# Attention and MLP in one kernel: batch 1's input is loaded earlier and its first work moved into the opening

## The chip, the cores and the metric

The kernel runs on one core of one Trainium2 chip. The time is device microseconds from the first to the last instruction of one execution, as the median of several runs; the profile is of one execution, whose span was 203.0 us.

## The reference

The inputs are `x` (8 batches, 8 heads, 512 rows, 64 columns), `state` (8 batches, 8 heads, 32 rows, 64 columns), and the weights `w_in` (512 x 2048) and `w_out` (2048 x 512), all float32. For each batch and head:

```
scores  = x @ state.T / 8            # 512 x 32
a       = softmax(scores)            # over the 32 state rows
xread   = a @ state                  # 512 x 64
scores2 = state @ x.T / 8            # 32 x 512
sread   = softmax(scores2) @ x       # 32 x 64
```

`xread` and `sread` are joined along the rows (544 rows a batch), the heads are laid side by side (512 columns), and the resulting 4352 x 512 matrix goes through an MLP with exact Gelu:

```
out = gelu(rows @ w_in) @ w_out      # 4352 x 512, float32
```

## The kernel before, in words

Everything is computed in bfloat16 with float32 sums. The eight batches follow one another; the order of all instructions on all engines is written out by hand, so each engine runs its instructions in exactly the order in which the program's lines issue them, and waits only for data and buffers.

For a batch `b`, `xtr` transposes x (64 columns of a head at a time, two heads into one 128-row tile) into `xT`. `state_prep` transposes the state and puts it in block form into `sbd`. `scores(b, half)` multiplies the two and takes exp on ScalarE into `e`; `norm` sums and divides on VectorE into `a`; `atr` transposes `a` into `AT`. Since `xread @ w_in` is `a @ (state @ w_in)`, the kernel first forms P = state @ w_in for 512 columns of w_in at a time (`p_mm`, then `p_copy`: one half is copied out of PSUM by ScalarE, the other by VectorE). A `burst` does `p_mm` for two or three such pieces and then their copies; `pmat` does one.

`M(k)` is one block of the first MLP layer: block `k % 16` of batch `k // 16`, 128 of the 2048 hidden columns for all 512 rows, two matmuls of 128x512 and a Gelu on ScalarE into `g`. `mm2_m(0, m)` and `U(u)` are pieces of the second layer, four matmuls of 128x512 each that add into the four output banks `op`. `mm2_m(0, m)` needs Gelu block `m` of batch 0 and rows `128 m` to `128 m + 127` of w_out. From batch 2 on, the second layer uses sums of operands (`g_sum`, `X`), which is not touched here.

`sread(b)` computes the second attention from the same `e` and from `xo`, a copy of x with columns of ones that give the softmax sums (`ones0` fills it for batch 0, `rearr_ones` for the others); `sread_out` divides on VectorE into `srm`; `srt` transposes that into `XSR`, where the state rows of all batches are gathered for the end of the kernel.

PSUM has eight banks. Four are the pool `ps_f`, handed out in turn for first-layer blocks `hp`, P pieces `p_ps`, transposes, scores `pt` and `sr`; the next user of a buffer waits until the last one's result has been copied out. The other four, `o0` to `o3` of `ps_o`, hold the output sums `op` and, in the opening, small things.

The loads of weights, of the states of batches 1 to 7 and of x of batches 1 to 7 are issued by GpSimd and convert float32 to bfloat16 on the way. Their order is that of the calls: `load_w_in`, `load_w_out` and `load_st` at the top, then `load_x(1)` in the middle of the opening, then `load_rest()`. x of batch 0 comes by other queues.

The opening (lines 955 to 1014) does attention and the first four blocks of batch 0 while the first weights arrive; `keep_warm` fills waits there with matmuls whose result nobody uses. `first` is the two halves of those four blocks, into the tiles `hps`. After them comes a list of units by hand, lines 1013 to 1096, in which batch 0's second layer is interleaved with batch 1's attention and first blocks, M(16) to M(31), and with batch 2's attention.

Of the kernel before, what the change touches and what calls it, by code (L numbers as in the profile page):

```python
# [10 lines left out]
BF16 = mybir.dt.bfloat16  # L11
# [6 lines left out]
def kernel(  # L18
# [17 lines left out]
    SJ = S // 128  # L36
# [11 lines left out]
    ps_f = ctx.enter_context(tc.tile_pool(name="ps_f", bufs=4, space=PSUM))  # L48
    ps_o = ctx.enter_context(tc.tile_pool(name="ps_o", bufs=1, space=PSUM))
# [51 lines left out]
    def load_w_in(f0, f1):  # L101
        for t in range(2):
            nc.gpsimd.dma_start(
                out=w_in_bf[64 * t:64 * t + 64, :, f0:f1],
                in_=moe_w_in[256 * t:256 * t + 256, f0:f1].rearrange("(c d) f -> d c f", c=HC),
            )
# [3 lines left out]
    def load_w_out(m0, m1):  # L110
        nc.gpsimd.dma_start(out=w_out_bf[:, m0:m1, :], in_=w_out_r[:, m0:m1, :])

    def load_x(b):
        xb = xin.tile([128, H, SJ * D], BF16, name="xb", tag="xb")
        nc.gpsimd.dma_start(out=xb, in_=xr[b])
        xbs[b] = xb

    def load_st(b0, b1):
        nc.gpsimd.dma_start(
            out=st_bf[:, b0:b1, :, :].rearrange("q b t d -> q (b t) d"),  # L120
            in_=st_rows[:, b0:b1, :, :].rearrange("q b t d -> q (b t) d"),
        )

    load_w_in(0, 256)
    load_w_in(256, 512)
    load_w_out(0, 2)
    load_st(1, 2)
    load_w_out(2, 4)
    load_w_in(512, 1024)

# [23 lines left out]
    def state_prep(b0, b1):  # L154
        n = b1 - b0
        ps = ps_f.tile([128, n, HC, NS], BF16, name="st_ps", tag="f")
        for b in range(b0, b1):
            nc.tensor.transpose(
                ps[:, b - b0, :, :].rearrange("p c n -> p (c n)"),
                st_bf[:, b, :, :].rearrange("q t d -> q (t d)"),  # L160
                ident,
            )
        for t in range(2):
            nc.vector.tensor_copy(
                out=sbd[64 * t:64 * t + 64, b0:b1, :, 32 * t:32 * t + 32].rearrange(
                    "d b c n -> d (b c) n"
                ),
                in_=ps[64 * t:64 * t + 64, :, :, :].rearrange("d b c n -> d (b c) n"),
            )
# [34 lines left out]
    def begin(b):  # L204
        A = Att()
        atts[b] = A
        A.x4 = x4s[b % 2]
        A.xo = xos[b % 2]
        if b > 0:
            A.xT = att.tile([128, SJ, HC, 128], BF16, name="xT", tag="xT")  # L210

    def begin_e(b):
        A = atts[b]
        A.e = att.tile([128, SJ * 2, HC * NS], BF16, name="e", tag="e")
        A.a = att.tile([128, SJ * 2, HC * NS], BF16, name="a", tag="a")
# [12 lines left out]
    def rearr_ones(b):  # L228
        A = atts[b]
        eng = nc.vector if b < 2 else nc.gpsimd  # L230
        src = xbs[b].rearrange("p (t c) (j d) -> p t c j d", t=2, d=D)
        for t in range(2):
            eng.tensor_copy(  # L233
                out=A.xo[:, :, :, 2 + 64 * t:66 + 64 * t].rearrange("p j c d -> p c j d"),
                in_=src[:, t],
            )
# [9 lines left out]
    def ones0(q):  # L246
        nc.vector.tensor_copy(
            out=atts[0].xo[:, :, q % 2 * 2:q % 2 * 2 + 2, 2 + q // 2 * 64:66 + q // 2 * 64],
            in_=x0b[:, q, :, :, :],
        )  # L250
# [8 lines left out]
        copy(out=xT0[:, q, :, :], in_=ps)  # L259


    def xtr(b, cs):
        A = atts[b]
        xv = xbs[b].rearrange("p (t c) (j d) -> p j c t d", t=2, d=D)
        ps = ps_f.tile([128, len(cs), SJ, 128], BF16, name="xT_ps", tag="f")
        for i, c in enumerate(cs):
            for j in range(SJ):
                for t in range(2):
                    nc.tensor.transpose(ps[64 * t:64 * t + 64, i, j, :], xv[:, j, c, t, :], ident)  # L269
        nc.vector.tensor_copy(  # L270
            out=A.xT[:, :, cs[0]:cs[0] + len(cs), :].rearrange("p j c n -> p c j n"), in_=ps
        )
# [47 lines left out]
    def scores(b, half):  # L320
        A = atts[b]
        if half == 0:
            begin_e(b)
        pt = ps_f.tile([128, SJ, 2, 2, NS], FP32, name="pt", tag="f")
        for ci in range(2):
            c = 2 * half + ci
            for j in range(SJ):
                nc.tensor.matmul(  # L328
                    pt[:, j, :, ci, :],
                    lhsT=A.xT[:, j, c, :],  # L330
                    rhs=sbd[:, b, c, :],
                    start=True,
                    stop=True,
                )
        nc.scalar.activation(  # L335
            out=A.e[:, :, 64 * half:64 * half + 64],
            in_=pt.rearrange("p j t c n -> p (j t) (c n)"),
            func=AF.Exp,
            scale=scale,
        )  # L340
# [40 lines left out]
    def sread(b):  # L381
        A = atts[b]
        A.sr = ftile([128, 2, 65], "sr")
        for t in range(2):
            for j in range(SJ):
                for c in range(HC):
                    nc.tensor.matmul(  # L387
                        A.sr[32 * c:32 * c + 32, t, :],
                        lhsT=A.e[:, 2 * j + t, 32 * c:32 * c + 32],
                        rhs=A.xo[:, j, c, 1 + 65 * t:66 + 65 * t],  # L390
                        start=(j == 0),
                        stop=(j == SJ - 1),
                    )

    def sread_out(b):
        A = atts[b]
        A.srm = att.tile([128, 2, D], BF16, name="srm", tag="srm")
        flat = A.sr.rearrange("q t d -> q (t d)")
        inv = att.tile([128, 2], FP32, name="inv", tag="inv")
        nc.vector.reciprocal(out=inv, in_=flat[:, 0:130:129])  # L400
        nc.vector.tensor_tensor(
            out=A.srm,
            in0=flat[:, 1:129].rearrange("q (t d) -> q t d", t=2),
            in1=inv[:, :].to_broadcast((128, 2, D)),
            op=ALU.mult,
        )

    def srt(b):
        A = atts[b]
        ps = ps_f.tile([128, HC, NS], BF16, name="srT", tag="f")  # L410
        nc.tensor.transpose(  # L411
            ps.rearrange("p c n -> p (c n)"), A.srm.rearrange("q t d -> q (t d)"), ident
        )
        nc.vector.tensor_copy(out=XSR[:, :, :, b], in_=ps)  # L414
# [29 lines left out]
    def burst(chunks, b_read=None):  # L444
        done = []
        first = len(chunks) < 4 and b_read is not None
        if first:
            sread(b_read)
        for i, (b, f) in enumerate(chunks):
            done.append((b, f, p_mm(b, f, ftile if i < 2 else otile)))  # L450
        for x in done[:2]:
            p_copy(*x)
        if b_read is not None and not first:
            sread(b_read)
        for x in done[2:3]:
            p_copy(*x)
        if b_read is not None:
            sread_out(b_read)
        for x in done[3:]:
            p_copy(*x)  # L460
# [65 lines left out]
    def mm2_m(b, m):  # L526
        for j in range(SJ):
            if m == 0:
                ops[b, j] = otile([128, d_model], "op")
            nc.tensor.matmul(  # L530
                ops[b, j],
                lhsT=gs[b][:, m, j * 128:(j + 1) * 128],
                rhs=w_out_bf[:, m, :],
                start=(m == 0),
                stop=(m == MC - 1),
            )
# [364 lines left out]
    def M(*ms):  # L901
        for m in ms:
            mm1(m // MC, m % MC)
# [70 lines left out]
    keep_warm(6)  # L974
    sums0(1)
    norm0(0)
    load_x(1)
    scores0(3)
    sums0(2)
    sums0(3)  # L980
# [22 lines left out]
    first(0, (0, 1))  # L1003
    atr(0, (1,))
    nc.vector.tensor_copy(out=Ps[0][:, 1, 256:512], in_=late[1])
    for q in range(4):
        ones0(q)
    first(0, (2, 3))
    first(1, range(4))
    for m in range(4):  # L1010
        nc.scalar.activation(out=gs[0][:, m, :], in_=hps[m], func=AF.Gelu)
    turn[0] = 3
    mm2_m(0, 0)
    mm2_m(0, 1)
    state_prep(1, 2)
    mm2_m(0, 2)
    burst([(1, 0), (0, 1)])
    mm2_m(0, 3)
    M(4, 5)
    M(6)  # L1020
    begin(1)
    xtr(1, (0, 1))
    xtr(1, (2, 3))
    sread(0)
    sread_out(0)
    M(7)
    scores(1, 0)
    scores(1, 1)
    srt(0)
    mm2_m(0, 4)  # L1030
    mm2_m(0, 5)
    rearr_ones(1)
    mm2_m(0, 6)
    norm(1, 0)
    sread(1)
    pmat(0, 2)
    sread_out(1)
    norm(1, 1)
    mm2_m(0, 7)
    M(8, 9)  # L1040
    M(10, 11)
    mm2_m(0, 8)
    atr(1)
    mm2_m(0, 9)
    burst([(1, 1), (0, 3)])
    mm2_m(0, 10)
    M(16, 17)
    M(12, 13)
    srt(1)
    M(14, 15)  # L1050
# [7 lines left out]
    U(13)  # L1058
    state_prep(2, B)
    U(14)  # L1060
    M(18, 19)
    U(15)
    burst([(2, 0), (2, 1), (2, 2)])
    U(16)
# [110 lines left out]
    b = B - 1  # L1175
# [40 lines left out]
```

The softmax here doesn't subtract the row's maximum and nothing guards it: scores larger than these inputs give would overflow.

## Time and profile before

| What | Value |
|---|---|
| Time, median of three runs | 204.88 us (204.70 to 205.03) |
| Span of the profiled execution | 203.0 us |
| Granted TensorE clock | 1.000 |
| VectorE busy | 149.1 us, 73% |
| ScalarE busy | 134.7 us, 66% |
| GpSimd busy | 67.0 us, 33% |
| Read from and written to HBM | 17.30 MB and 8.91 MB |

Busy time of an engine is the time that its instructions were in work, and the share is of the span. PE is TensorE's matmuls, PEld its weight loads, which overlap them. In the page's second part the span is cut into 40 slices of 5.1 us, and a digit is the busy share of a slice in tenths. In a list of instructions, `out<-in` names the tiles, and what stands in brackets at the end of a line is how long the engine sat idle before it and what ended that. The end of a matmul is modelled, so its start is the better mark. For a load, the time to landing counts from its issue. Lines L530 and L515 are the second layer's matmuls (`mm2_m` and `mm2`), L995 and L489 the first layer's, L424 P, L269 the transposes of x, L387 `sread`, L328 the scores, L158 and L411 the transposes of the state and of `srm`.

### The profile page before, as it was taken

What the parts mean: (1) busy time and instruction counts of PE and PEld (TensorE: products, weight loads), DVE (VectorE), ACT (ScalarE), POOL (GpSimd) and SP (SyncE); (2) the same over time, 40 slices, a digit from 0 to 9 for tenths busy, and PEclk for the clock granted to TensorE, in tenths of its full rate; (3) what the DMA queues carried; (4) which work ended last, traced back from release to release, by engine and by line L of the source; (5) the groups of instructions that cost most, each with busy time, mean ns of one, the idle gap of its engine ahead of it and who ended that gap; (6) DMA issues with size and microseconds to landing.
All of it is one profiled execution on the core that took longest, in us unless ns stands there. A gap on an engine that the chain in (4) does not pass through costs nothing.

```text
span 203.0 us, 4784 instructions
## 1 busy us (share of the span) xinstructions
PE 198.0 (98%) x1987; PEld 128.1 (63%) x1987; DVE 149.1 (73%) x246; ACT 134.7 (66%) x237; POOL 67.0 (33%) x73
## 2 busy tenths in 40 slices
PE   7899999999999999999999999999999999999994
PEld 2444544444454577766776677667776787878893
DVE  2954863866767679877897787768778988895883
ACT  3785678479894879666967697587847576864120
POOL 8963610742860315370626602430220002200000
PEclk9999999999999999999999999999999999999999
DMA  6999999789475908952693405380109001040225
GB/s 194 196 178 203 207 197 192 121 236 179 83 95 149 224 0 105 158 171 38 77 182 116 93 3 120 107 140 3 52 0 194 15 3 52 3 155 0 55 98 162
DMA packets 40325, 23.14 MB, mean 114 GB/s; under 512 B 21872, under 2 KB 38384, under 8 KB 40304
## 3 DMA queue, kind: packets, MB, share of 16 engines
q1 hardware_dynamic: 25616, 14.36, 29.6%
q0 software_dynamic: 14000, 8.10, 29.2%
q10 hardware_dynamic: 688, 0.39, 0.6%
q8 instruction: 15, 0.25, 0.5%
q14 instruction: 6, 0.05, 0.1%
HBM read 17.30 MB, written 8.91 MB: 129 GB/s over the span
## 4 chain that ended last, share of the span: by engine, by line
PE 94%; DMA 2%; DVE 1%; ACT 1%; issue 0%
PE xp L585 35%; PE hp L489 27%; PE op L515 9%; PE op L530 5%; PE p_ps L424 4%; PE sp L791 3%; PE rp L857 3%; PE xp L696 2%; DMA st_f<-in_state_dram 2%; PE pt L328 2%; PE sr L387 1%; PE hp L995 1%; PE aT_ps L369 1%; PE xT_ps L269 0%; DVE x0b L241 0%; PE warm_ps L148 0%
## 5 line engine op out<-in xcount | busy, mean ns | idle before, releaser
L496 ACT ACTIVATE g<-hp 128x512 bf16<-128x512 f32 x124 | 66.9, 602 | 28.4 <-PE hp L489 23.0
L489 PE MATMUL hp<-AT,P 128*128 128x512 bf16 x248 | 63.2, 379 | 0.0
L585 PEld LDWEIGHTS <-gsum 128*128 128x128 bf16 x448 | 43.3, 98 | 10.4 <-issue 1.9
L579 DVE TENSOR_TENSOR gsum<-g 128x2048 bf16<-128x2048 bf16 x30 | 38.7, 1305 | 0.1
L489 PEld LDWEIGHTS <-P 128*128 128x128 bf16 x248 | 22.8, 98 | 21.9 <-issue 2.2
L585 PE MATMUL xp<-ws,gsum 128*128 128x256 bf16 x256 | 30.6, 273 | 0.0
L436 DVE CAST P<-p_ps 128x512 bf16<-128x512 f32 x31 | 20.0, 684 | 5.4 <-PE p_ps L424 5.4
L585 PE MATMUL xp<-ws,g 128*128 128x256 bf16 x192 | 22.9, 273 | 0.0
L585 PE MATMUL xp<-w_out_bf,gsum 128*128 128x256 bf16 x192 | 22.8, 273 | 0.0
L435 ACT CAST P<-p_ps 128x512 bf16<-128x512 f32 x31 | 16.8, 597 | 7.2 <-PE p_ps L424 6.3
L585 PEld LDWEIGHTS <-g 128*128 128x128 bf16 x192 | 18.8, 98 | 4.1
L639 POOL TENSOR_TENSOR u<-s,oh 128x512 f32<-128x512 f32 x5 | 6.6, 1315 | 41.1 <-ACT oh L636 41.1
L515 PE MATMUL op<-w_out_bf,g 128*128 128x512 bf16 x80 | 19.7, 379 | 0.0
L233 POOL COPY xo<-xb 128x1024 bf16<-128x1024 bf16 x12 | 15.5, 1325 | 12.6 <-PE sr L387 12.6
L223 POOL COPY x<-xb 128x1024 bf16<-128x1024 bf16 x12 | 12.3, 1055 | 8.9 <-DMA xb<-in_x_dram 8.9
L604 POOL TENSOR_TENSOR v<-q,oh 128x512 f32<-128x512 f32 x5 | 7.2, 1431 | 20.4 <-ACT oh L641 20.4
L515 PEld LDWEIGHTS <-g 128*128 128x128 bf16 x80 | 7.6, 98 | 9.3 <-issue 0.8
L348 DVE TENSOR_REDUCE cs<-e 128x16 f32<-128x512 bf16 x14 | 9.5, 678 | 4.5 <-ACT e L335 4.5
L530 PE MATMUL op<-w_out_bf,g 128*128 128x512 bf16 x48 | 11.8, 380 | 0.0
L351 DVE TENSOR_TENSOR a<-e,ics 128x512 bf16<-128x512 bf16 x14 | 10.3, 735 | 0.5
L414 DVE COPY XSR<-srT 128x128 bf16<-128x128 bf16 x8 | 5.7, 758 | 6.6 <-PE srT L411 6.6
L424 PE MATMUL p_ps<-w_in_bf,sbd 64*32 64x512 bf16 x248 | 10.1, 382 | 0.0
(127 smaller groups left out, 234.7 us busy)
## 6 DMA issues: line engine op xcount, KB each, us to landing
xb<-in_x_dram POOLq DMA_DIRECT2D x7, 512.0 KB, 6.0
out_dram<-oh SPq DMA_DIRECT2D x13, 256.0 KB, 2.5
out_dram<-osb SPq DMA_DIRECT2D x10, 256.0 KB, 3.3
out_dram<-oh SPq DMA_DIRECT2D x5, 512.0 KB, 2.7
w_out_bf<-in_moe_w_out_dram POOLq DMA_DIRECT2D x8, 256.0 KB, 10.0
w_in_bf<-in_moe_w_in_dram POOLq DMA_DIRECT2D x6, 256.0 KB, 10.4
x0f<-in_x_dram SPq DMA_DIRECT2D x3, 256.0 KB, 4.1
w_in_bf<-in_moe_w_in_dram POOLq DMA_DIRECT2D x4, 128.0 KB, 4.5
```

The source lines that it names most:

```text
L223: nc.gpsimd.tensor_copy(out=A.x4[:, :, :, 64 * t:64 * t + 64].rearrange("p j c d -> p c j d"), in_=src[:, t],)
L233: eng.tensor_copy(out=A.xo[:, :, :, 2 + 64 * t:66 + 64 * t].rearrange("p j c d -> p c j d"), in_=src[:, t],)
L351: nc.vector.tensor_tensor(out=A.a[:, :, hs].rearrange("p g (c n) -> p g c n", n=NS), in0=e4, in1=ics[:, :, :].to_broadcast((128, G, 2, NS) ...
L424: nc.tensor.matmul(ps[t][32 * c:32 * c + 32, :], lhsT=sbd[64 * t:64 * t + 64, b, c, 32 * t:32 * t + 32], rhs=w_in_bf[64 * t:64 * t + 64, c ...
L435: nc.scalar.copy(out=dst[:, 0, :], in_=ps[0])
L436: nc.vector.tensor_copy(out=dst[:, 1, :], in_=ps[1])
L489: nc.tensor.matmul(hp, lhsT=Ps[b][:, t, m * 128:(m + 1) * 128], rhs=atts[b].AT[:, :, t, :], start=(t == 0), stop=(t == 1),)
L496: nc.scalar.activation(out=gs[b][:, m, :], in_=hp, func=AF.Gelu)
L515: nc.tensor.matmul(ps, lhsT=gs[b][:, m, j * 128:(j + 1) * 128], rhs=w_out_bf[:, m, :], start=(m == 0), stop=(m == MC - 1),)
L530: nc.tensor.matmul(ops[b, j], lhsT=gs[b][:, m, j * 128:(j + 1) * 128], rhs=w_out_bf[:, m, :], start=(m == 0), stop=(m == MC - 1),)
L579: nc.vector.tensor_tensor(out=t, in0=g_q(b, h0, k0), in1=g_q(b, h1, k1), op=op)
L585: nc.tensor.matmul(ps[:, j - js[0], :], lhsT=lhs[:, m, 128 * j:128 * j + 128], rhs=rhs[:, m, :], start=(first and j == js[0] and m == 0), ...
```

## The change

It brings batch 1's attention forward. x of batch 1 is loaded right behind the first 512 columns of w_in, ahead of the first rows of w_out. Its transposes and those of its state are issued before batch 0's second layer begins, one of the two groups of transposes through the bank `o2` of the other pool; its scores come after two units of the second layer instead of after seven blocks. Batch 1's normalisation and `atr` follow earlier, so that its first blocks, M(16) to M(19), can run among batch 0's, as other work to put between the units of the second layer. `sread(0)`, its division and two of the `ones0` copies move with it. No instruction is added or left out.

```diff
     load_w_in(0, 256)
     load_w_in(256, 512)
+    load_st(1, 2)
+    load_x(1)
     load_w_out(0, 2)
-    load_st(1, 2)
     load_w_out(2, 4)
     load_w_in(512, 1024)
...
-    def xtr(b, cs):
+    def xtr(b, cs, pool=ps_f, tag="f"):
...
-        ps = ps_f.tile([128, len(cs), SJ, 128], BF16, name="xT_ps", tag="f")
+        ps = pool.tile([128, len(cs), SJ, 128], BF16, name="xT_ps", tag=tag)
...
     norm0(0)
-    load_x(1)
     scores0(3)
...
-    for q in range(4):
-        ones0(q)
+    ones0(0)
+    ones0(1)
     first(0, (2, 3))
     first(1, range(4))
     for m in range(4):
         nc.scalar.activation(out=gs[0][:, m, :], in_=hps[m], func=AF.Gelu)
+    begin(1)
+    xtr(1, (0, 1), ps_o, "o2")
+    xtr(1, (2, 3))
+    state_prep(1, 2)
+    ones0(2)
+    ones0(3)
     turn[0] = 3
     mm2_m(0, 0)
     mm2_m(0, 1)
-    state_prep(1, 2)
+    scores(1, 0)
+    scores(1, 1)
     mm2_m(0, 2)
+    sread(0)
+    sread_out(0)
     burst([(1, 0), (0, 1)])
+    norm(1, 0)
     mm2_m(0, 3)
     M(4, 5)
-    M(6)
-    begin(1)
-    xtr(1, (0, 1))
-    xtr(1, (2, 3))
-    sread(0)
-    sread_out(0)
-    M(7)
-    scores(1, 0)
-    scores(1, 1)
-    srt(0)
+    M(6, 7)
+    norm(1, 1)
     mm2_m(0, 4)
     mm2_m(0, 5)
     rearr_ones(1)
+    srt(0)
     mm2_m(0, 6)
-    norm(1, 0)
+    atr(1)
     sread(1)
     pmat(0, 2)
     sread_out(1)
-    norm(1, 1)
     mm2_m(0, 7)
+    M(16, 17)
     M(8, 9)
     M(10, 11)
     mm2_m(0, 8)
-    atr(1)
+    M(18, 19)
     mm2_m(0, 9)
     burst([(1, 1), (0, 3)])
     mm2_m(0, 10)
-    M(16, 17)
     M(12, 13)
     srt(1)
     M(14, 15)
...
     U(14)
-    M(18, 19)
     U(15)
```

## The prediction

> **What bounds the kernel now.** I read the page first, then the chain of waits in order of time, then the timeline of the first 45 us, then the loads one by one.
>
> The page says that one engine carries the span:
>
> ```profile
> PE 198.0 (98%) x1987; PEld 128.1 (63%) x1987; DVE 149.1 (73%) x246; ACT 134.7 (66%) x237; POOL 67.0 (33%) x73
> ...
> PE   7899999999999999999999999999999999999994
> ```
>
> TensorE is full from the third slice to the last. The change neither adds nor removes a matrix instruction, so the time can only move by what TensorE idles. The chain of waits for the stretch that the diff touches (start, length, what):
>
> ```profile
> 12.29 1.04 PE hp L995 x4
> ...
> 13.35 1.90 PE op L530 x8
> 15.25 0.06 PE st_ps L158
> 15.31 0.86 PE op L530 x4
> 16.17 0.56 PE p_ps L424 x16
> 16.73 0.97 PE op L530 x4
> ...
> 17.70 1.51 PE hp L489 x6
> 19.21 1.01 PE xT_ps L269 x32
> ```
>
> A 128x512 matmul costs 0.216 us in a stream (`op x4` is 0.86). From 12.29 us on, every piece starts where the one before ends. What idle there is hides in pieces that are too long (six matmuls are 1.30 us, the piece of `hp` is 1.51), and the timeline gives it with its releaser in brackets:
>
> ```profile
> 13.35 1.41 PEld L530 LDWEIGHTS <-g 128*128 128x128 bf16 x8 [0.53 <-ACT g L1011]
> ...
> 17.70 0.10 PEld L489 LDWEIGHTS <-P 128*128 128x128 bf16 x1 [0.50 <-ACT P L435]
> ...
> 21.22 0.29 DVE L401 TENSOR_TENSOR srm<-sr,inv 128x128 bf16<-128x128 f32 x1
> 21.56 0.10 PEld L411 LDWEIGHTS <-srm 128*128 128x128 bf16 x1
> ...
> 27.69 0.54 PEld L530 LDWEIGHTS <-g 128*128 128x128 bf16 x4 [0.41 <-ACT g L496]
> ```
>
> In lost stream time (start minus the start of the matmul before, minus 0.216) these are: 0.20 us at 13.35 (the first Gelu), 0.21 at 17.70 (P of the burst still being copied), 0.14 at 21.57 (the transpose of srm), 0.08 at 27.7 and 0.04 at 33.7. So 0.67 us is all that any reordering can win in this stretch; from 34 us to the end I find only the 0.1 us steps at each change of tile shape.
>
> The loads are the second resource. Slices 1 to 8 of the page move about 200 GB/s, and each load's issue and time to landing can be had one at a time, here those of w_out blocks 2 and 3 and of x of batch 1:
>
> ```profile
> L111 POOL DMA_DIRECT2D w_out_bf<-in_moe_w_out_dram x1: 753/753/753, 7.1 to 7.1; - x1
> DMA to landing us min/median/max: 6.4/6.4/6.4
> ...
> L115 POOL DMA_DIRECT2D xb<-in_x_dram x1: 962/962/962, 9.0 to 9.0; - x1
> DMA to landing us min/median/max: 9.6/9.6/9.6
> ```
>
> Issue plus landing, in order: w_in 256-512 at 9.6 and 10.3 us, w_out 0-1 at 11.6, state 1 at 11.8, w_out 2-3 at 13.5, w_in 512-1024 at 14.8 and 16.0, x1 at 18.6, w_out 4-5 at 19.9, 6-7 at 21.3. They land one after another, 256 KB per 1.3 us: a line in which order is everything.
>
> **What the Trainium skill says.** *DMA: Bandwidth & Descriptors*, "Issuing engines are not separate DMA queues": all loads end on the same 16 engines. The trace agrees: landings follow the order of issue, 1.3 us apart. *PSUM — Partial Sum Buffer*, "Engine vs sequencer instructions": Scalar and Vector queues are strict FIFO and matmuls start in program order; so a matmul that waits holds all behind it, as at 17.70. *ScalarE: Activation LUTs*, "What ACT_TABLE_LOAD costs": about 1283 ns a load, the same as the 1283 ns here.
>
> **The change part by part.**
>
> *Load order.* x1 (512 KB) goes ahead of w_out 0-1, w_out 2-3 and w_in 512-1024. x1 now ends at the byte position (512 + 32 + 512 KB) at which w_out 2-3 ended before: 13.5 us. By rate it is 10.3 + 0.2 (state) + 2.6 (x1's own, 18.6 minus 16.0) = 13.1. I take 13.3 and keep both ends. The three it overtakes come 2.6 later at most, and less by the same token: w_out 0-1 at 14.6 (1.3 behind x1), w_out 2-3 at 15.9, w_in 512-1024 at 18.6, the place that x1 leaves. Loads behind these don't move.
>
> *Transposes in the opening.* `first` ends streaming at 13.15, and TensorE would wait for Gelu until 13.35. Now it waits for x1 until 13.35, transposes for 0.9 us (19.14 to 20.01 before), then the state with 0.15 of shape change and work: 14.4. w_out 0-1 is there at 14.65. `mm2_m(0,0)` and `(0,1)` take 8 x 0.216 = 1.73, to 16.38. Hidden by that: VectorE's two xT copies (0.645 each, from 14.0), two sbd copies (0.47), the last two `ones0` (0.48), done at 16.3. The o2 bank that the first transposes borrow is free again at 14.7, when `op` 3 needs it 0.65 after 14.65.
>
> *Scores early.* 16 matmuls, 0.47 (44.60 to 45.07 at the later `pt`), to 16.85; `mm2_m(0,2)` 0.86, to 17.71. The table load for exp starts when the fourth Gelu ends (14.8) and is over by 16.1, before `pt` is full: free.
>
> *sread(0) ahead of the burst.* It starts at 17.80 after the 0.09 shape change and takes 0.36, as at 24.32; P of (1,0) 0.22, to 18.38. P of (0,1) now has two waits. It needs w_in 512-1024: 18.65. And it needs its second PSUM buffer: the four `f` buffers go round, and by my count (transpose, state, two `pt`, `sr`, then two for (1,0), two for (0,1)) its second is that of `sr`, which is free when `sread_out` is done: about 0.5 after 17.80 for the matmuls, 0.19 and 0.29 for the two VectorE rows, 0.05 to release: 18.83. So both waits end within 0.2 us of each other and TensorE loses 0.45. Everything else of batch 0 stands behind that matmul. Then 0.22 + 0.09: `mm2_m(0,3)` at 19.14.
>
> *Balance there.* Before, `mm2_m(0,3)` began at 16.66, without the transposes and sread (19.05 to 20.52, 1.47) and the scores (0.47): 18.60 for equal work. The new order is **0.54 behind**.
>
> *After it.* What comes back: P of (1,0) is copied during the new wait, so M(4) no longer waits (0.21); srm is long done when `srt(0)` comes (0.14); the Gelus at 27.7 and 33.7 have run ahead (0.12). Together **0.47 back**. What is new: `mm2_m(0,4)` meets the Gelu of block 4, since ScalarE does two P copies to 19.6, a table load of 1.28, then Gelu from 20.9 to 21.5: 0.05 at most. M(17) needs the `sr` buffer of batch 1: 0.04. And the burst of (1,1) and (0,3) is now followed by one `mm2_m` and then M(12), which reads P of (0,3); M(16) and M(17) stood between. That is the layout of the burst at 16.1, which cost 0.21 at 17.70. Together **0.30**. VectorE from 19.7 does two norms (1.6 each), `rearr_ones` (0.96), XSR (0.35), two AT copies (0.38) and ends at 25.4, just before P of (0,2) needs the buffer: no wait by my figures, but with little to spare.
>
> *M(18), M(19) earlier* moves 1.73 us of work within a stream that has no gap on either side: zero. The rest of the program is unchanged and full.
>
> Sum: 0.54 - 0.47 + 0.30 = **+0.37 us: 205.25**.
>
> **Rivals.**
> - *The loads set the pace* (x1 lands at 13.5 to 14.0, or the buffers come back later than I count). Each 0.1 us of x1 is 0.1 us at the end, since all that follows in the opening is tied to it: +0.2 to +0.7 on top, and a miss at P of (0,2) up to 0.4: 205.9. For it: the equal byte position at 13.5, and a rate that falls to 158 GB/s between 11.0 and 13.4 us. Against: x1 itself took 2.6 us for 512 KB before, the full rate.
> - *Hidden after all:* x1 at 13.1 and the wait of M(12) shortened because ScalarE is ahead: 0.37 - 0.2 - 0.15 = 0, 204.9.
> - *Faster:* (0,1) doesn't wait, because its buffer is another one and w_in lands by 18.3, and M(12) doesn't either: 0.37 - 0.45 - 0.21 - 0.2 = -0.5, 204.4. It needs every tight place to turn out well; 0.67 is the ceiling.
>
> **How the numbers follow.** The forecast case (205.0 to 205.6) has 0.50, the loads' rival 0.20, hidden 0.17, faster 0.13. The bound of 0.2% is 0.41 us: slower begins at 205.29, which cuts the forecast case in half: slower 0.25 + 0.20 = 0.45; same 0.25 + 0.17 = 0.42; faster 0.13. The range runs from 204.5 to 206.0.
>
> **What would show it.** Right: the transposes start at about 13.3, `op` at 14.7, the second half of the burst after a hole of some 0.4 near 18.5, M(12) after a hole of 0.2, and from 40 us on the old picture shifted by 0.3 to 0.4. Wrong: no hole at the burst, x1 past 13.6, or a hole near 25 us at P of (0,2).

## The result, and the profile after

| | Before | Changed |
|---|---|---|
| Median | 204.94 us (204.70 to 205.03, 4 runs) | 207.29 us (206.14 to 207.68, 4 runs) |
| Ratio of the times | | 1.0107, interval 1.0065 to 1.0150 |
| Span of the profiled execution | 203.0 us | 205.8 us |

The change costs about 1.1%, outside the predicted range of 204.5 to 206.0. A ratio, here and below, leaves out a run more than 1.5% above the fastest of its kernel, which is one run of all (210.50, in s2). The page of the changed kernel shows at once where: busy time of TensorE by slice, its granted clock, and what the loads moved, in 40 slices of 5.1 us.

```profile
PE   7599999999999999999999999999999999999994
...
PEclk9979999999999999999999999999999999999999
...
GB/s 199 153 172 195 204 204 188 93 275 110 163 23 134 261 47 60 153 135 119 27 177 79 178 3 75 79 207 2 54 0 182 25 3 51 3 153 0 54 92 165
```

Slice 2 has lost busy time (5 where it had 8), slice 3 some clock, and the loads move 153 and 172 GB/s in slices 2 and 3 where they moved 196 and 178. From slice 4 on TensorE is as full as before, as far as tenths show. So nearly all of it is decided before 15 us. The chain of waits (start, length, what) says by what; line numbers of the changed kernel are one higher than before (L531 for L530), those of the variants up to seven:

```profile
1.75 6.87 DMA x0f<-in_x_dram
8.62 0.02 issue
8.64 0.44 DVE x0b L242
...
14.55 1.02 PE hp L995 x4
15.58 1.08 PE xT_ps L270 x32
16.65 0.18 PE st_ps L159
16.83 0.02 issue
16.85 1.90 PE op L531 x8
```

The last quarter of batch 0's x is in after 6.87 us, at 8.6 us, and its cast (L242) runs then; before, it ran at 6.94:

```profile
6.94 0.45 DVE L241 CAST x0b<-x0f 128x512 bf16<-128x512 f32 x1
```

TensorE stood still meanwhile, and then ran at half clock:

```profile
5.00:7.00 2.00, 1.94 (x21) 1.30 (x20) 1.62 (x5) 1.40 (x5) 2.00 (x4) 1.00 1.31 204
7.00:9.00 2.00, 0.20 (x4) 0.08 (x4) 0.36 (x2) 0.79 (x3) 1.74 (x3) 1.00 1.29 140
9.00:11.00 2.00, 1.80 (x24) 0.94 (x25) 1.76 (x6) 0.77 (x2) 1.72 (x3) 0.74 1.15 134
11.00:13.00 2.00, 2.00 (x15) 0.75 (x15) 1.92 (x5) 1.22 (x3) 1.59 (x3) 0.50 1.31 166
```

Here a line is a stretch and its length, then the busy time of TensorE, its weight loads, VectorE, ScalarE and GpSimd with the count of instructions, then the clock, the share of time that packets took on the 16 load engines (over 1 where packets overlap) and GB/s. TensorE stands still for 1.92 us, from 7.20 to 9.12, and has clock 0.50 for 3.41 us, from 9.96 to 13.37. The Trainium skill (*TensorE: Matmul & The Clock Gate*, "What's actually happening") states that the clock is halved after at least one idle window of about 3.4 us. This trace agrees in kind, but 1.92 us of standing still were enough. The second half of `first`, at 12.29 us before, begins at 14.55: 2.26 us later, for a cast that was 1.70 later.

The transposes of batch 1's x come next, and their first weight load waits for that x ("x1" from here on), which landed at 15.53:

```profile
15.57 0.92 PEld L270 LDWEIGHTS <-xb 128*64 128x64 bf16 x32 [0.49 <-DMA xb<-in_x_dram]
```

So two delays end together here: with `first` on time, and x1 where it was, TensorE would have waited for x1 until the same moment.

That is one execution. Two more profiles of the same kernel, below, have the quarter of batch 0's x in time and are still slow. The experiments take the two delays apart.

### The profile page after: what moved, and what is told of

Same layout as the page of the kernel before. It is cut to its first block, busy times and chain, and to the rows that moved or that the text cites. A ratio compares the mean times of both kernels' runs of the same rounds, so it can differ in the third digit from the quotient of the medians.

```text
span 205.8 us, 4783 instructions
## 1 busy us (share of the span) xinstructions
PE 199.3 (97%) x1987; PEld 129.0 (63%) x1987; DVE 149.1 (72%) x246; ACT 134.6 (65%) x237; POOL 66.4 (32%) x73
## 3 DMA queue, kind: packets, MB, share of 16 engines
HBM read 17.30 MB, written 8.91 MB: 127 GB/s over the span
## 4 chain that ended last, share of the span: by engine, by line
PE 93%; DMA 3%; DVE 1%; SPq 0%; issue 0%
PE xp L586 34%; PE hp L490 26%; PE op L516 8%; PE op L531 5%; PE p_ps L425 4%; DMA x0f<-in_x_dram 3%; PE sp L792 3%; PE rp L858 3%; PE xp L697 2%; PE pt L329 2%; PE sr L388 1%; PE hp L995 1%; PE warm_ps L149 1%; PE aT_ps L370 1%; PE xT_ps L270 1%; SPq L90 0%
## 5 line engine op out<-in xcount | busy, mean ns | idle before, releaser
L234 POOL COPY xo<-xb 128x1024 bf16<-128x1024 bf16 x12 | 15.5, 1325 | 12.6 <-PE sr L388 12.6
L531 PE MATMUL op<-w_out_bf,g 128*128 128x512 bf16 x48 | 11.9, 380 | 0.0
L425 PE MATMUL p_ps<-w_in_bf,sbd 64*32 64x512 bf16 x248 | 10.6, 382 | 0.1
L352 DVE TENSOR_TENSOR a<-e,ics 128x512 bf16<-128x512 bf16 x14 | 10.3, 735 | 0.5
```

Of the source, the lines that this page charges most:

```text
L234: eng.tensor_copy(out=A.xo[:, :, :, 2 + 64 * t:66 + 64 * t].rearrange("p j c d -> p c j d"), in_=src[:, t],)
L352: nc.vector.tensor_tensor(out=A.a[:, :, hs].rearrange("p g (c n) -> p g c n", n=NS), in0=e4, in1=ics[:, :, :].to_broadcast((128, G, 2, NS) ...
L425: nc.tensor.matmul(ps[t][32 * c:32 * c + 32, :], lhsT=sbd[64 * t:64 * t + 64, b, c, 32 * t:32 * t + 32], rhs=w_in_bf[64 * t:64 * t + 64, c ...
L531: nc.tensor.matmul(ops[b, j], lhsT=gs[b][:, m, j * 128:(j + 1) * 128], rhs=w_out_bf[:, m, :], start=(m == 0), stop=(m == MC - 1),)
```

## The experiments

Each kernel's profile is read at five marks (us; start, or landing for a load):

```
                      2nd half   x1       trans-   first   first
                      of first   landed   poses    op      xp
before                12.29      18.66    19.14    13.35   68.58
predicted             12.29      13.3     13.35    14.65   68.95
changed               14.55      15.53    15.57    16.85   71.30
r1 changed again      12.50      14.45    14.50    15.77   70.22
s2 changed, third     12.42      13.92    13.97    15.26   69.79
e1 state early        12.18      19.0     19.03    13.24   68.47
e2 state late         11.81      14.04    14.09    15.66   70.11
e3 loads only         12.38      14.79    23.64    16.18   73.08
e4 waits for x0       12.04      14.22    14.27    15.86   70.32
r2 x1 in two loads    12.23      12.72    13.18    14.27   69.31
r3 x1 behind w_out    11.72      15.95    15.99    17.93   74.20
r4 one piece a row    11.93      12.21    12.88    13.97   69.08
s1 x1 in four loads   12.34      13.42    13.29    15.78   70.41
t1 w_in one chunk     13.70      14.54    14.66    15.85   70.30
s3 srt later          12.27      19.56    19.60    13.33   69.05
```

`xp` is the first matmul of batch 2's second layer, the first with operand sums. Behind it nothing of the change is left, so its distance from 68.58 is what the change cost in that execution; the predicted value is 68.58 + 0.37.

### First set: which load makes what late

**e1**, the kernel before:

```diff
     load_w_in(256, 512)
+    load_st(1, 2)
     load_w_out(0, 2)
-    load_st(1, 2)
     load_w_out(2, 4)
```

> The kernel before with one edit: the 32 KB load of batch 1's state one place earlier, ahead of w_out 0-1, where the changed kernel has it; x of batch 1 stays late. Marker: the start of the second half of `first` (12.29 us before, 14.55 in the changed kernel). Theory A (x1's early load makes the last quarter of batch 0's x late): marker 12.3, time 204.9 within 0.3. Theory B (the state's small pieces do it): marker 13 or later, time 205.6 or more.

Measured: marker 12.18; 205.34 us (204.70 to 206.24, 20 runs), ratio 1.0018 (1.0006 to 1.0030). In this profile nothing late shows at `xp`. A cost of 0.2% remains over the runs, and the profile, which is of the fastest run, doesn't show of what.

**e2**, the changed kernel:

```diff
     load_w_in(256, 512)
-    load_st(1, 2)
     load_x(1)
     load_w_out(0, 2)
+    load_st(1, 2)
     load_w_out(2, 4)
```

> The changed kernel with the state's load put back behind w_out 0-1; x of batch 1 stays early. Theory A: marker 13 or later, time 206.0 to 207.7. Theory B: marker 12.3, and the rest as worked out, 205.0 to 205.6. Theory C (the late quarter is chance, and not tied to what is queued behind w_in): marker moves freely, 205 to 207.

Measured: marker 11.81, and yet 205.72 us (205.22 to 206.47, 7 runs), ratio 1.0049 (1.0030 to 1.0067). This fits none of the three as written; in time B comes closest. Batch 0's x is in time, half a microsecond better than before, and `xp` is 1.53 late all the same. x1 lands at 14.04 where I had 13.3, and then the load that was moved, the state, holds TensorE and with it `op`, to 15.66:

```profile
15.59 0.10 PEld L159 LDWEIGHTS <-st_bf 128*128 128x128 bf16 x1 [0.58 <-DMA st_bf<-in_state_dram]
```

The profile is of one of the two slowest of the seven runs, at 206.33. Over the runs, moving these 32 KB alone about halves the loss (5 of the 7 runs are under 206.00, and none of the changed kernel's 16 runs is), so the place of the state's load may be part of the cause; no profile here shows how.

**e3**, the kernel before with the changed loads:

```diff
     load_w_in(256, 512)
+    load_st(1, 2)
+    load_x(1)
     load_w_out(0, 2)
-    load_st(1, 2)
     load_w_out(2, 4)
...
-    load_x(1)
     scores0(3)
```

> The kernel before with the changed order of loads alone, all other instructions in the old order. Theories A and B: marker 13 or later, and on top the burst at 16 us now waits for w_in 512-1024 until 18.6: 207.0 to 209.5. Rival (the new order of instructions, not of loads, delays the opening): marker 12.3, time 207 from the burst's wait alone.

Measured: marker 12.38, 209.58 us (209.04 to 211.07, 4 runs), ratio 1.0241 (1.0198 to 1.0283). Batch 0's x is in time, against A and B, and the loss is well above the rival's 207. In the old order of instructions nothing covers the weights that x1 pushes back: `mm2_m(0,0)` waits for w_out until 16.18, and after these 2.78 us of standing still the clock is 0.50 for 3.41 us. The reordering of instructions is thus a repair of what the reordering of loads costs, and it repairs more than half.

**e4**, the changed kernel:

```diff
     load_w_in(256, 512)
+    nc.gpsimd.tensor_copy(out=hold, in_=x0f[:, 3, 1, 0:1])
     load_st(1, 2)
     load_x(1)
```

> The changed kernel, with GpSimd copying one element of the last quarter of batch 0's x before it issues the two early loads, so that both are queued only once that quarter is there. Theories A and B: marker 12.3 to 12.5; x1 lands at about 14, 0.5 later than worked out for the changed kernel: 205.2 to 206.0, with a spread of 0.4 or less. Rival (something else in the changed kernel delays it): marker 13 or later, 206.5 or more.

Measured: marker 12.04, as A and B have it, but 206.66 us (206.55 to 207.45, 4 runs), ratio 1.0099 (1.0074 to 1.0124). With batch 0's x safe the kernel is as slow as ever. The test isn't a clean one: the copy holds back the issue of x1 to 7.38 us, from 6.40, and the loads move only 63 and 82 GB/s from 8 to 10 us. But r1 and s2 below, without an edit, say the same: the late quarter, conspicuous as it is, isn't the main cost. Theories A, B and C are all about that quarter.

### Second set: why x1 lands late

**r1** is the changed kernel without an edit.

> The changed kernel as it is, on the chip of the three below. Theory D (x1's 1024 small pieces reach the DMA engines late: with only w_in ahead of it the engines run dry at 8 to 10 us, and x1 lands at 14 or later): DMA rate near 100 GB/s between 8 and 10 us, x1 lands 14.0 to 15.6. Theory A again (batch 0's last quarter late): marker (second half of `first`) 13 or later. If both happen in some executions only: marker 12 to 14.6, times 206.1 to 207.7, wider than before's.

Measured: 207.04 us (206.07 to 208.94, 4 runs), ratio 1.0119 (1.0058 to 1.0180). The chain of this execution starts from x1 and from nothing else:

```profile
6.44 8.02 DMA xb<-in_x_dram
14.45 0.04 issue
14.50 1.08 PE xT_ps L270 x32
15.58 0.18 PE st_ps L159
15.76 0.01 issue
15.77 1.90 PE op L531 x8
```

and the weight loads of TensorE name the same two waits, for x1 and, short, for w_out:

```profile
14.49 0.92 PEld L270 LDWEIGHTS <-xb 128*64 128x64 bf16 x32 [1.47 <-DMA xb<-in_x_dram]
...
15.76 0.33 PEld L531 LDWEIGHTS <-g 128*128 128x128 bf16 x3 [0.16 <-DMA w_out_bf<-in_moe_w_out_dram]
```

x1 took 8.0 us from issue, and part of the reason can be seen in the rate, the last number of each line. Before:

```profile
8.00:9.00 1.00, 1.00 (x19) 0.43 (x16) 0.93 (x4) 0.74 (x3) 1.00 (x2) 1.00 1.20 185
9.00:10.00 1.00, 0.87 (x8) 0.40 (x7) 1.00 (x3) 0.71 (x3) 1.00 (x3) 1.00 1.44 191
```

r1:

```profile
8.00:9.00 1.00, 0.93 (x21) 0.41 (x17) 0.87 (x3) 0.48 (x2) 1.00 (x3) 1.00 1.30 127
9.00:10.00 1.00, 0.87 (x12) 0.30 (x11) 0.96 (x3) 0.92 (x3) 1.00 (x3) 1.00 1.00 113
```

Between the end of w_in and the run of x1 the rate is low for two microseconds (the hole, from here on); it is back at 190 GB/s only from 11 us on. The two aren't alike. From 8 to 9 us the share, 1.30, is no lower than before, 1.20; what differs are the packets, 249 of them before, 457 and small in r1:

```profile
DMA packets 457, 0.13 MB, mean 127 GB/s; under 512 B 269, under 2 KB 457, under 8 KB 457
```

The state's load, the one ahead of x1, is cut into 256 pieces of 128 B. From 9 to 10 us the share falls too, to 1.00 from 1.44: there less is under way. In e2, with the state behind w_out 0-1, the rate is 118 and 168 GB/s in these two microseconds, and x1 landed at 14.04.

**r2**, the changed kernel, in `load_x` for batch 1 alone:

```diff
-        nc.gpsimd.dma_start(out=xb, in_=xr[b])
+        for t in range(2):
+            nc.gpsimd.dma_start(
+                out=xb[:, 4 * t:4 * t + 4, :], in_=xr[b][:, 4 * t:4 * t + 4, :]
+            )
```

> The changed kernel, x of batch 1 loaded by two loads of four heads (512 pieces each) one behind the other. Theory D, if the lateness grows with the pieces of one load: the gap at 8 to 10 us shrinks, second half lands by 13.6, mm2_m(0,3) starts 0.3 or more earlier than in the changed kernel when measured from the second half of `first`; 205.3 to 206.2. Rival E (the place in the queue, whatever is loaded there): x1 lands 14.0 to 15.5, 206.2 to 207.5.

Measured: 205.80 us (205.54 to 206.65, 8 runs), ratio 1.0051 (1.0032 to 1.0069). The same bytes in the same pieces land at 12.72, and more than half of the loss is gone; 5 of the 8 runs are under 206.00:

```profile
8.00:9.00 1.00, 0.95 (x16) 0.41 (x14) 0.93 (x4) 0.74 (x2) 1.00 (x2) 1.00 1.56 164
9.00:10.00 1.00, 0.92 (x7) 0.38 (x6) 1.00 (x3) 0.66 (x3) 1.00 (x3) 1.00 1.31 170
```

TensorE no longer waits for x1: the transposes begin at 13.18, right behind `first`. From the second half of `first` to `mm2_m(0,3)` it is 7.21 us, against 7.84 in r1, but 6.87 in the changed kernel's first profile, where x1 was hidden by the late `first`.

**r3**, the changed kernel:

```diff
     load_st(1, 2)
-    load_x(1)
     load_w_out(0, 2)
+    load_x(1)
     load_w_out(2, 4)
```

> The changed kernel with x of batch 1 one place later, behind w_out 0-1. Theory D: the 256 KB of w_out (256 pieces) hide the wait for x1's pieces: no hole under 150 GB/s between 8 and 10 us, x1 lands at 14.2 to 14.6, no later than in e2 and e4 although 256 KB more lie ahead of it, and w_out 0-1 at about 11.8; 205.5 to 206.3. Rival E: the hole stays at 8 to 10 us and x1 lands at 15 or later, 206.5 or more.

Measured: 210.02 us (209.56 to 210.76, 4 runs), ratio 1.0251 (1.0212 to 1.0289). E's landing and time came true (x1 at 15.95), but neither theory's place of the hole. The hole isn't hidden by w_out, as D wanted; and it doesn't stay at 8 to 10 us, as E wanted. It moves along with x1:

```profile
8.00:9.00 1.00, 0.87 (x15) 0.30 (x10) 0.93 (x3) 0.87 (x3) 1.00 (x2) 1.00 1.48 176
9.00:10.00 1.00, 0.98 (x14) 0.48 (x14) 0.97 (x4) 0.57 (x2) 1.00 (x3) 1.00 1.03 151
10.00:11.00 1.00, 0.79 (x6) 0.30 (x7) 0.71 (x2) 0.98 (x3) 1.00 (x2) 1.00 0.79 96
```

TensorE stands still for 3.25 us until x1 is there, and the clock is 0.50 for 6.83 us from 14.79 on; that is in the 210.02 too.

**r4**, the changed kernel, in `load_x` for batch 1 alone:

```diff
-        nc.gpsimd.dma_start(out=xb, in_=xr[b])
+        flat = x[1].rearrange("h s d -> (h s d)").rearrange("(p f) -> p f", p=128)
+        nc.gpsimd.dma_start(out=xb.rearrange("p h f -> p (h f)"), in_=flat)
```

> The changed kernel with x of batch 1 read as one flat run of 2048 numbers for each of the 128 partitions instead of eight runs of 256: the same bytes at the same place in the queue, in an order of elements that is not that of the reference, so this kernel's batch 1 is not computed on the right rows. Theory D: few pieces, no hole at 8 to 10 us, x1 lands at 13.0 to 13.4, transposes at 13.4, mm2_m(0,3) at 19.2, time 205.0 to 205.7. Rival E: x1 at 14.0 or later, 206 to 207.5.

Measured: 205.45 us (205.22 to 206.57, 12 runs), ratio 1.0043 (1.0027 to 1.0060); 8 of the 12 runs are under 206.00. The load puts batch 1's numbers into other places than the reference has them, so this kernel measures the load and is of no other use.

```profile
8.00:9.00 1.00, 0.87 (x16) 0.50 (x15) 0.93 (x3) 0.79 (x4) 1.00 (x2) 1.00 1.42 168
9.00:10.00 1.00, 1.00 (x15) 0.39 (x13) 0.96 (x4) 0.57 (x3) 1.00 (x3) 1.00 1.09 198
```

No hole; x1 at 12.21, 1.1 earlier than I had it; `mm2_m(0,3)` at 19.20, where the prediction has 19.14; the profiled execution took 205.33. With x1 in time the new order still loses 0.4%, about the time that I predicted, and the timeline shows the place of loss that I predicted, the second half of the burst:

```profile
17.47 0.12 PEld L429 LDWEIGHTS <-sbd 64*32 64x32 bf16 x9
...
18.83 0.14 PEld L429 LDWEIGHTS <-sbd 64*32 64x32 bf16 x7 [1.24 <-DVE P L441]
...
19.20 0.55 PEld L535 LDWEIGHTS <-g 128*128 128x128 bf16 x4 [0.23 <-issue]
```

The wait is put down to a VectorE copy that ended at 18.74. The second half of w_in 512-1024 landed at 18.73, and TensorE needs that here, not the copy: in the changed kernel the same matmul ran at 21.08 while the same copy went on until 21.63. It is the wait that the prediction has at 18.65. So x1's gain of 1.1 us is spent on waiting for w_in.

### Third set: how far pieces and loads explain it

**s1**, as r2 with four loads of two heads.

> The changed kernel, x of batch 1 in four loads of two heads (256 pieces each). If what counts is the number of pieces of one load (two loads landed at 12.7, one load at 14.5 to 15.5): x1 all there by 12.7 or before, transposes at 13.2 or before, and then the old second wait for w_in 512-1024 at 18.6 to 19.0 keeps mm2_m(0,3) at 19.1 to 19.5: 205.3 to 206.0, no better than two loads. Rival (issuing four loads costs GpSimd 0.7 us each and pushes the weights back): w_in 512-1024 at 19.5 or later, 206 to 207.

Measured: 206.63 us (206.44 to 207.24, 4 runs), ratio 1.0079 (1.0059 to 1.0099). x1 is there at 13.42, but now w_out 0-1 behind it comes only at 15.73, 2.3 us later instead of 1.3. The hole has moved behind the first half of x1:

```profile
8.00:9.00 1.00, 1.00 (x19) 0.42 (x18) 0.94 (x3) 0.73 (x3) 1.00 (x2) 1.00 1.63 176
9.00:10.00 1.00, 0.67 (x14) 0.42 (x7) 0.99 (x3) 0.77 (x3) 1.00 (x3) 1.00 1.34 178
10.00:11.00 1.00, 0.78 (x13) 0.34 (x11) 0.93 (x4) 0.81 (x2) 1.00 (x3) 1.00 1.03 124
11.00:12.00 1.00, 0.99 (x8) 0.43 (x7) 0.51 (x2) 0.98 (x2) 1.00 (x3) 1.00 0.99 122
```

So the expectation, no better than two loads, holds only as a bound. The rival's figures are those that came: the four issues take GpSimd 2.85 us, w_out 0-1 is issued at 9.25 instead of 7.34 in r1, and w_in 512-1024 is complete at 20.06.

**t1**, the changed kernel:

```diff
-    load_w_in(0, 256)
-    load_w_in(256, 512)
+    load_w_in(0, 512)
```

> The changed kernel with the first 512 columns of w_in loaded as one chunk: the same 512 KB ahead of x of batch 1, in two loads of 256 pieces of 1 KB instead of four of 256 pieces of 512 bytes. If the pieces queued ahead of x1 count (1280 before it in the changed kernel, 768 here): no hole at 8 to 10 us, x1 lands by 13.3, mm2_m(0,3) near 19.2, 205.2 to 206.0, if P of batch 0 is not itself late for the larger first chunk (about 8.9 instead of 7.4). Rival (x1's own load of 1024 pieces is late wherever it stands): the hole stays, x1 lands at 14 or later, 206.2 or more.

Measured: 206.01 us (205.14 to 207.84, 12 runs), ratio 1.0071 (1.0042 to 1.0099). x1 lands at 14.54 and the hole stays (148 and 99 GB/s from 8 to 10 us). Fewer pieces ahead of x1 don't help, which speaks for the rival; in this profile the larger chunk of w_in was itself late (10.60) and TensorE stood still for it, so the test isn't a clean one.

**s2**, the changed kernel once more.

> The changed kernel once more, for the last quarter of batch 0's x, which was 2 us late in one of two profiles. If it is late in about every second execution: runs in two groups, some above 207.3 with a mean clock of 0.992, some at 206 to 206.6; if it was a rare event: all at 206 to 206.7.

Measured: 206.98 us (206.00 to 210.50, 8 runs), ratio 1.0101 (1.0065 to 1.0136); three runs at 208.46, 208.82 and 210.50 with mean clocks of 0.991, 0.990 and 0.984, five at 206.00 to 207.29 with 0.999 or 1.000. Over its 16 runs the changed kernel has six with a clock of 0.992 or less, all at 207.5 or above. In these sets no run of the kernel before fell under 0.998. A stretch of 3.41 us at half clock makes a mean of 0.992 over 206 us, and two make 0.984. The one profile of the changed kernel with such a stretch is the one with batch 0's x late. What it was in the other five isn't shown: all four runs of e3 and of r3 have a clock of 0.992 or less, and in their profiles batch 0's x is in time and TensorE stands still for w_out or x1.

**s3**, the kernel before:

```diff
     scores(1, 1)
-    srt(0)
     mm2_m(0, 4)
...
     M(10, 11)
+    srt(0)
     mm2_m(0, 8)
```

> The kernel before with srt(0) issued behind M(10) and M(11) instead of behind the scores, which takes away the one wait of 0.14 us that the changed order removes without any load. Expected 204.74, that is 0.1 to 0.2 less than before, at the edge of what can be told; rival: the buffer that srt then takes turns a wait up elsewhere, 204.9 or more.

Measured: 205.14 us beside 205.11 for the kernel before, ratio 0.9994 (0.9979 to 1.0010): no difference that can be told, where 0.1 to 0.2 us less was expected. In the profiled execution x1, in its late place, landed at 19.56 and TensorE stood still for 0.4 us ahead of its transposes; the scatter of the loads is larger than what this edit can win.

## Why the prediction was wrong

**The step that failed is the landing of x1**: "By rate it is 10.3 + 0.2 (state) + 2.6 (x1's own, 18.6 minus 16.0) = 13.1. I take 13.3 and keep both ends." It landed at 13.92, 14.45 and 15.53 in three profiles of the changed kernel; the prediction's own sign of being wrong, x1 past 13.6, came true in all three. The term that was mis-sized is x1's own. Behind the state's load, which was complete at 9.61, 9.72 and 11.19, x1 took 4.31, 4.73 and 4.34 us, where 2.6 was put. That 2.6 was read where x1 stood behind six weight loads and the line was full. In the changed order the line is not full: ahead of x1 the rate fell to between 91 and 133 GB/s for two microseconds. r4 and r2 change only how x1 is loaded, give it back in time, and take the loss from 1.1 or 1.2% to 0.4 or 0.5%.

The rule that the prediction gave for such a case, "Each 0.1 us of x1 is 0.1 us at the end", held: x1 was 0.62, 1.15 and 2.23 us past 13.3, and `xp` 0.84, 1.27 and 2.35 us past the predicted 68.95.

**The loads that x1 overtakes** came late with it. w_in 512-1024, for which I had 18.6, was complete at 20.65 in the changed kernel, 19.56 in r1 and 19.44 in s2. And "Loads behind these don't move" failed: w_out 4-5, at 19.9 before, landed at 21.93, 20.84 and 20.69.

**"`first` ends streaming at 13.15"** was assumed, not examined. In one of three profiles it came 2.26 us later, because a part of batch 0's x was late and the clock then fell. The prediction's rival "the loads set the pace" was the right kind of case, with too small a number (x1 at 13.5 to 14.0) and a chance of 0.20. A small slip of reading: of the slices said to move about 200 GB/s, the eighth moves 121.

What was right can be measured against its own start, with the lengths between the marks (us):

```
                   first    transposes  op to       mm2_m(0,3)
                   to tr.   to op       mm2_m(0,3)  to xp
predicted          1.06     1.30        4.49        49.81
changed            1.02     1.28        4.57        49.88
r1 changed again   2.00     1.27        4.57        49.88
s2 changed, third  1.55     1.29        4.65        49.88
r4 one piece       0.95     1.09        5.23        49.88
```

In the changed kernel's first profile every length after `first` is within 0.1 us of the working: late as x1 was, `first` was about as late. All of the 2.72 us at `xp` is the 2.26 of `first` plus 0.46, for which I had 0.37. In r1 and s2 the loss is instead the first length, 2.00 and 1.55 for 1.06: the wait for x1. (In s2 `mm2_m(0,3)` is taken from its first weight load, at 19.91.) In r4 both lengths are better than worked out, and the burst pays by waiting for w_in; that the sum came out as predicted is in part these two making up for each other.

Step by step: the wait in the burst came where it was put, and by the cause that was named second. In the changed kernel it is the buffer of `sr`, as the timeline of its weight loads has it (start, length, what, and in brackets the wait ahead and its releaser):

```profile
21.08 0.11 PEld L425 LDWEIGHTS <-sbd 64*32 64x32 bf16 x7 [0.60 <-DVE srm L402]
...
24.09 1.41 PEld L531 LDWEIGHTS <-g 128*128 128x128 bf16 x8 [0.40 <-ACT g L497]
25.62 0.10 PEld L412 LDWEIGHTS <-srm 128*128 128x128 bf16 x1
...
35.74 0.10 PEld L490 LDWEIGHTS <-P 128*128 128x128 bf16 x1 [0.50 <-ACT P L436]
```

The first line is the wait in the burst. The second is `mm2_m(0,4)` meeting its Gelu: 0.08 us of stream lost, 0.05 forecast. The third, the transpose of `srm`, has no wait in brackets any more: the 0.14 that was to come back did. The last is M(12) behind the second burst: 0.21 forecast, 0.17 lost at its start and 0.03 at the matmul after. P of (0,2), feared as a miss, doesn't wait. Moving M(18) and M(19) cost nothing, as said.

**What stays open**: why the rate falls ahead of x1. That a large count of pieces in one load is part of it fits the runs (one load of 1024 has the hole in every early place tried; two loads of 512, or one piece a row, don't), but it isn't shown: four loads of 256 have the hole later, and they are also issued later; fewer pieces ahead of x1 don't remove it; e2 halves the loss with the 1024 pieces in one load; and the kernel before has a weaker hole at 11 to 13 us where no x is moving. The hole isn't all of the lateness either. The trace keeps 16 partial landings of each load, and eight of x1's were in by 12.1 to 12.5 us in the three profiles; the rest of the delay is in the last few.

The late quarter of batch 0's x is of another kind. In that profile 15 of its 16 shares were in by 6.25 us and the last at 8.62; the weight loads moving at that time show the same, the first with 15 shares in by 6.78 and the last at 8.91, and so does x1, with 14.11 and 15.53. One packet of the hardware queue, between 6 and 7 us, took 7.9% of 16 engines for 1 us, which is 1.26 us:

```profile
q1 hardware_dynamic: 1, 0.00, 7.9%
```

In r1 the four packets there took 1.2% together. This reads as one load engine held up for some 2 us, which made both batch 0's x and part of x1 late; the trace doesn't name the engine, and no variant's profile has it.

The medians aren't accounted for in full. The profiled executions of r1 and s2, 206.44 and 206.00, are at the lower end of their runs, and what the slower runs with a full clock waited for isn't known.

No version tried beats the kernel before.

## What to carry to other kernels

When a transfer is moved forward, work out the whole line again from its issue on, and ask whether the line is full at the new place: a landing read off a full stretch need not hold elsewhere, and here it was 0.6 to 2.2 us too early. Where TensorE has no gaps, an earlier load can win no more than the few tenths of waits that are left, and it pushes back every load that it overtakes; price those first. And take more than one profile of a slow result before explaining it: the first one here showed the most striking wait, and two others were slow without it.

## What the runs showed of the hardware

- The order of loads, and the way in which one is cut, moved landings by 2 us: 512 KB at the same place landed at 12.2 (one piece a row), 12.7 (two loads), 13.4 (four) and 13.9 to 15.5 us (one load of 1024 pieces). The first three are from one profile each.
- A load counts as landed with the last of its 16 shares, and the shares lie far apart: of x1 in r1 they run from 11.83 to 14.45 us, with the middle at 12.26; five come after 13.0. Before, in a full line, x1's ran from 16.80 to 18.66.
- Standing still for 1.92 us (changed), 2.78 (e3) and 3.25 (r3) was followed by TensorE at half clock for 3.41, 3.41 and 6.83 us; 1.82 us in t1, and 1.21 to 1.26 in e2, e4 and s1, were not. In the changed kernel's first profile this made 2.26 us out of a cast that was 1.70 late.
